# A 16-byte constant tile moved in front of the activations in SBUF

## The chip, the cores and the metric

One core of one Trainium2 chip. The metric is the device time of one execution in microseconds, lower is better; before the change the median of three runs is 929.96 us (928.1 to 932.1).

## The reference

A retention (linear attention) layer followed by two feed-forward layers, all in float32:

```python
scores = scale * np.matmul(q, k.transpose(0, 1, 3, 2))      # q, k, v: 4 x 8 x 576 x 64
ret = scores * Dmat[None]                                   # gamma[h] ** (i - j) for i >= j, else 0
x = np.matmul(ret, v)                                       # heads joined: x is 2304 x 512
h = x @ w_in;  g = np.maximum(0.01 * h, h);  x = g @ w_out      # first layer, d_ff = 2048
h = x @ w_in;  g = h - np.tanh(h);           x = g @ w_out      # second layer, own weights
```

## The kernel before

Everything lies in SBUF with 128 partitions. The activations are x, transposed, as two tensors: xh is x rounded to the matmul type fp32r, xl is what the rounding left. Each holds four slices (kk) of 128 features by 2304 tokens. The weights are split into a high and a low half in the same way, and so is g, the output of the elementwise part. One product therefore costs three matmuls: high x high, high x low, low x high.

The kernel first does the retention, in 16 pairs of heads, and fills xh and xl; meanwhile it already starts the first layer on narrow blocks of tokens. Then come the layers. Each has 16 slices of d_ff, in four groups of four; for a group the token blocks (four of 512 tokens and one of 256) are gone through, and for each block the four slices f. One (block, slice) is a step; there are 164 steps, 124 of them with 512 tokens. A step has

- `h_mm` (L181): 12 matmuls, over four kk and three pairs (w high, xh), (w high, xl), (w low, xh), all into one PSUM bank h. x is the moving operand, 512 or 256 columns; the weights of the ring are the stationary one.
- the elementwise part: `act_a` (L193, or L201 to L207 in the second layer) and `chain` (L215, or L218 to L222), then the split of g by ScalarE (L224) and GpSimd (L225).
- `o_mm` (L251): 12 matmuls of 512 columns into four PSUM banks, three for each, done LAG = 2 steps later. In the first layer g moves and the weights are stationary, in the second the weights move and g is stationary (there a block of 256 tokens takes 6 matmuls of 512 columns).
- after the fourth slice, `evac` (L276, L274): VectorE adds the banks to acc. At the end of a layer acc is split into xh and xl again (L280, L281), or stored.

The order of all instructions is written out by hand; in the loop of the layers a step issues h_mm(s), chain(s - 1), act_a(s), o_mm(s - 2), and between them the loads, the conversion of the next group's weights (lines 124 to 162) and the evictions. Within an engine the order is that of the code.

SBUF is laid out in the order in which tiles are taken from the pools. The pool `keep` comes first and holds xh, xl, acc and qb. xh, xl and acc have 36,864 bytes in each partition, 72 times 512. qb has 16 bytes in a slot of 32; it holds four constants that ScalarE's L204 and L207 use as bias. Behind `keep` come the ring of split weights (`wring`, two tags of four tiles of 4,096 bytes), the staging tiles, and the pools of a stage, with g in tiles of 4,096 bytes. In bytes from the partition's start:

```
tile          before   by 512      after   by 512
qb           127,104      128     16,512      128
xh            16,512      128     16,544      160
xl            53,376      128     53,408      160
acc           90,240      128     90,272      160
weight ring  127,136      160    127,136      160
g (layers)   188,576      160    188,576      160
```

Of the kernel before, what the change touches and what calls it, by code (L numbers as in the profile page):

```python
# [10 lines left out]
F32 = mybir.dt.float32  # L11
# [7 lines left out]
P = 128  # L19
# [14 lines left out]
def retention_moe_moe(  # L34
# [28 lines left out]
    keep = ctx.enter_context(tc.tile_pool(name="keep", bufs=1))  # L63
    wring = ctx.enter_context(tc.tile_pool(name="wring", bufs=GF))
    stage = ctx.enter_context(tc.tile_pool(name="stage", bufs=2))

    xh = keep.tile([P, KK, NT], F32R, name="xh")
    xl = keep.tile([P, KK, NT], F32R, name="xl")
    acc = keep.tile([P, KK * NT], F32, name="acc")
    acc_t = acc.rearrange("p (d t) -> p d t", d=KK)  # L70
    acc_n = acc.rearrange("p (t e) -> p t e", e=DM)
    qb = keep.tile([P, 4], F32, name="qb")

# [614 lines left out]
```

## Time and profile before

| | |
|---|---|
| median of three runs | 929.96 us (928.1 to 932.1) |
| the profiled execution's own time | 927.96 us |
| its span, first to last instruction | 926.1 us |
| mean granted clock of TensorE | 0.992 |
| PE busy | 886.5 us (96%), 4832 matmuls |
| VectorE, ScalarE, GpSimd busy | 597.6, 388.0, 468.5 us |
| HBM traffic | 57 MB, 62 GB/s over the span |

Times in the profile are those of one execution, from the span's start. PE is TensorE's matmuls, PEld its weight loads, DVE VectorE, ACT ScalarE, POOL GpSimd. A matmul's end is modelled and matmuls overlap in the records, so the pace of matmuls is read from the differences of their starts, not from durations. The chain of waits is followed back from the last instruction, at each step to what released it.

### The profile page before, as it was taken

What the parts mean: (1) busy time and instruction counts of PE and PEld (TensorE: products, weight loads), DVE (VectorE), ACT (ScalarE), POOL (GpSimd) and SP (SyncE); (2) the same over time, 40 slices, a digit from 0 to 9 for tenths busy, and PEclk for the clock granted to TensorE, in tenths of its full rate; (3) what the DMA queues carried; (4) which work ended last, traced back from release to release, by engine and by line L of the source; (5) the groups of instructions that cost most, each with busy time, mean ns of one, the idle gap of its engine ahead of it and who ended that gap; (6) DMA issues with size and microseconds to landing.
All of it is one profiled execution on the core that took longest, in us unless ns stands there. A gap on an engine that the chain in (4) does not pass through costs nothing.

```text
span 926.1 us, 12850 instructions
## 1 busy us (share of the span) xinstructions
PE 886.5 (96%) x4832; PEld 739.7 (80%) x4832; DVE 597.6 (65%) x988; ACT 388.0 (42%) x777; POOL 468.5 (51%) x364
## 2 busy tenths in 40 slices
PE   5777999999999999999999999999999999999998
PEld 5677888888888888888888787888888877888886
DVE  5887656656573655546762677758785877755544
ACT  2343332233222322233334555675456455575554
POOL 3544422245223523354646855586557645595444
PEclk9989999999999999999999999999999999999999
DMA  7654421211110011101110011101110011001111
GB/s 276 212 174 150 155 99 47 91 46 46 46 63 30 24 46 69 45 1 46 46 69 24 23 46 69 47 0 46 47 69 24 23 46 69 1 1 46 45 46 69
DMA packets 21662, 58.36 MB, mean 63 GB/s; under 512 B 2528, under 2 KB 2912, under 8 KB 21600
## 3 DMA queue, kind: packets, MB, share of 16 engines
q1 hardware_dynamic: 21024, 57.16, 17.9%
q8 instruction: 38, 0.62, 0.3%
q10 hardware_dynamic: 576, 0.38, 0.1%
q14 instruction: 24, 0.20, 0.1%
HBM read 52.81 MB, written 4.72 MB: 62 GB/s over the span
## 4 chain that ended last, share of the span: by engine, by line
PE 60%; DVE 17%; POOL 11%; issue 6%; ACT 5%; DMA 1%; DVEq 0%; POOLq 0%; ACTq 0%
PE a L251 29%; PE h L181 28%; POOL v L203 5%; POOL g L225 4%; DVE v L219 4%; DVE v L222 3%; ACT g L224 2%; DVE acc L276 2%; DVE st L430 2%; DVE pt L396 2%; PE o L459 2%; POOL wp L162 1%; DVE cw L139 1%; ACT xh L468 1%; DVE cw L134 1%
## 5 line engine op out<-in xcount | busy, mean ns | idle before, releaser
L181 PE MATMUL h<-xh,wp 128*128 128x512 f32 (+1 forms) x1216 | 377.0, 375 | 0.0
L181 PEld LDWEIGHTS h<-xh,wp 128*128 128x128 f32 x1216 | 223.2, 188 | 45.2
L181 PE MATMUL h<-xl,wp 128*128 128x512 f32 (+1 forms) x608 | 228.3, 375 | 0.0
L251 PE MATMUL a<-wp,g 128*128 128x512 f32 x864 | 213.4, 393 | 5.2 <-POOL g L225 5.0
L251 PE MATMUL a<-g,wp 128*128 128x512 f32 (+1 forms) x1008 | 216.3, 364 | 1.9 <-POOL g L225 1.9
L225 POOL TENSOR_TENSOR g<-a,g 128x512 fp32r<-128x512 f32 (+1 forms) x84 | 107.7, 1283 | 197.8 <-ACT g L224 197.8
L251 PEld LDWEIGHTS a<-g,wp 128*128 128x128 f32 x1008 | 173.6, 192 | 32.3 <-POOL g L225 2.1
L251 PEld LDWEIGHTS a<-wp,g 128*128 128x128 f32 x864 | 160.9, 188 | 43.8 <-POOL g L225 9.2
L225 POOL TENSOR_TENSOR g<-v,g 128x512 fp32r<-128x512 f32 (+1 forms) x80 | 104.0, 1299 | 142.2 <-ACT g L224 142.2
L181 PEld LDWEIGHTS h<-xl,wp 128*128 128x128 f32 x608 | 114.7, 189 | 22.2
L162 POOL TENSOR_TENSOR wp<-cw,wp 128x512 fp32r<-128x512 f32 x64 | 90.4, 1421 | 55.1 <-ACT wp L161 54.6
L145 DVE SCALAR_TENSOR_TENSOR cw<-st,cw 128x512 uint32<-128x512 uint32 x128 | 116.1, 907 | 3.0
L224 ACT ACTIVATE g<-v 128x512 fp32r<-128x512 f32 (+1 forms) x80 | 47.2, 590 | 163.6 <-DVE v L222 162.5
L193 ACT ACTIVATE a<-h 128x512 f32<-128x512 f32 (+1 forms) x72 | 40.4, 562 | 172.0 <-PE h L181 172.0
L215 DVE TENSOR_TENSOR a<-h,a 128x512 f32<-128x512 f32 (+1 forms) x72 | 46.3, 643 | 101.0 <-ACT a L193 101.0
L203 POOL TENSOR_TENSOR v<-t,u 128x512 f32<-128x512 f32 (+1 forms) x80 | 101.9, 1273 | 11.9 <-ACT t L202 11.8
L276 DVE TENSOR_TENSOR acc<-a,acc 128x512 f32<-128x512 f32 (+1 forms) x114 | 72.0, 659 | 51.9 <-PE a L251 51.8
L219 DVE SCALAR_TENSOR_TENSOR v<-q,v 128x512 f32<-128x512 f32 (+1 forms) x80 | 58.3, 728 | 59.0 <-POOL v L203 58.0
L218 DVE TENSOR_TENSOR h<-h,t 128x512 f32<-128x512 f32 (+1 forms) x80 | 51.2, 640 | 48.4 <-ACT t L202 48.4
L224 ACT ACTIVATE g<-a 128x512 fp32r<-128x512 f32 (+1 forms) x84 | 47.9, 570 | 80.7 <-DVE a L215 80.7
L139 DVE TENSOR_SCALAR cw<-cw 128x512 uint32<-128x512 uint32 x64 | 63.4, 991 | 1.5
L222 DVE COPY_PREDICATED v<-mk,h 128x512 f32<-128x512 uint32 (+1 forms) x80 | 55.1, 688 | 8.2
(56 smaller groups left out, 745.9 us busy)
## 6 DMA issues: line engine op xcount, KB each, us to landing
st<-in_w1i SPq DMA_DIRECT2D x16, 512.0 KB, 3.3
st<-in_w1o SPq DMA_DIRECT2D x16, 512.0 KB, 3.3
st<-in_w2i SPq DMA_DIRECT2D x16, 512.0 KB, 3.2
st<-in_w2o SPq DMA_DIRECT2D x16, 512.0 KB, 3.2
kv<-in_vn SPq DMA_DIRECT2D x16, 320.0 KB, 4.3
qk<-in_qT SPq DMA_DIRECT2D x16, 288.0 KB, 2.9
qk<-in_kT SPq DMA_DIRECT2D x16, 288.0 KB, 3.4
out<-acc SPq DMA_DIRECT2D x18, 256.0 KB, 2.1
```

The lines of the kernel that those rows point to most:

```text
L139: nc.vector.tensor_scalar(out=t["w"], in0=t["w"], scalar1=3, scalar2=0x3FFFFFF8, op0=ALU.logical_shift_left, op1=ALU.bitwise_and,)
L145: nc.vector.scalar_tensor_tensor(out=t["w"], in0=t[src], scalar=scalar, in1=t["w"], op0=op, op1=ALU.bitwise_or)
L162: nc.gpsimd.tensor_tensor(out=wp[:, 1, :], in0=wf, in1=wp[:, 0, :].bitcast(F32), op=ALU.subtract)
L181: nc.tensor.matmul(out=ps[:, :n], lhsT=w[:, wi, cs], rhs=x[:, kk, t0:t0 + n], start=kk == 0 and i == 0, stop=kk == KK - 1 and i == 2,)
L203: nc.gpsimd.tensor_tensor(out=v[:, :n], in0=t_[:, :n], in1=u[:, :n], op=ALU.mult)
L218: nc.vector.tensor_tensor(out=h, in0=h, in1=t_, op=ALU.subtract)
L219: nc.vector.scalar_tensor_tensor(out=v, in0=q, scalar=RHO_A, in1=v, op0=ALU.add, op1=ALU.mult)
L222: nc.vector.copy_predicated(out=v, mask=mk.bitcast(U32), data=h)
L224: nc.scalar.activation(out=gt[:, 0, :n], in_=v, func=AF.Copy)
L225: nc.gpsimd.tensor_tensor(out=gt[:, 1, :n], in0=v, in1=gt[:, 0, :n].bitcast(F32), op=ALU.subtract)
L251: nc.tensor.matmul(out=o, lhsT=l, rhs=r, start=f == 0 and i == 0 and d % pack == 0, stop=f == GF - 1 and i == 2 and (d + 1) % pack == 0, s ...
L276: nc.vector.tensor_tensor(out=dst, in0=a, in1=dst, op=ALU.add)
```

## The change

qb is taken from the pool first instead of last. Nothing else changes: same instructions, same order, same waits. xh, xl and acc begin 32 bytes further on, qb begins where xh began, and all that lies behind the pool keeps its place.

```diff
+    qb = keep.tile([P, 4], F32, name="qb")
     xh = keep.tile([P, KK, NT], F32R, name="xh")
     xl = keep.tile([P, KK, NT], F32R, name="xl")
     acc = keep.tile([P, KK * NT], F32, name="acc")
     acc_t = acc.rearrange("p (d t) -> p d t", d=KK)
     acc_n = acc.rearrange("p (t e) -> p t e", e=DM)
-    qb = keep.tile([P, 4], F32, name="qb")
```

## Rows read from the trace of the kernel before

**Rows 1.** The page: busy time of PE and others; clock by slices.
```profile
PE 886.5 (96%) x4832; PEld 739.7 (80%) x4832; DVE 597.6 (65%) x988; ACT 388.0 (42%) x777; POOL 468.5 (51%) x364
...
PEclk9989999999999999999999999999999999999999
```

**Rows 2.** The chain by line, three stretches: 152 to 300, 528 to 775, 773 to 926.
```profile
by line: PE a L251 50.2%; PE h L181 49.9%
...
by line: POOL v L203 18.6%; POOL g L225 12.7%; DVE v L219 12.5%; DVE v L222 11.3%; issue 11.0%; ACT g L224 8.0%; PE a L251 6.2%; PE h L181 4.8%; DVE acc L276 4.1%; POOL wp L162 3.1%; DVE cw L139 1.6%; DVE h L218 1.4%; DVE cw L134 1.1%; DVE 
...
by line: PE a L251 47.2%; PE h L181 46.7%; POOL g L225 1.7%; DVE acc L276 0.9%; POOL v L203 0.5%; issue 0.4%; ACT q L204 0.3%; ACT mk L207 0.3%; ACT u L201 0.3%; ACT g L224 0.2%; ACT t L202 0.2%; ACTq L201 0.0%; POOLq L225 0.0%
```

**Rows 3.** The chain, in order of time: start us, us, what. Hand-overs.
```profile
495.62 2.75 DVE acc L276 x4
...
535.34 2.79 PE a L251 x11
...
554.75 1.44 PE h L181 x12
...
773.33 1.43 PE a L251 x5
```

**Rows 4.** Timeline of PE, 402 to 410.5: start us, us, instructions merged.
```profile
402.04 2.91 PE L251 MATMUL a<-g,wp 128*128 128x512 f32 x12
404.78 0.40 PE L181 MATMUL h<-xh,wp 128*128 128x512 f32 x1
...
407.58 2.91 PE L251 MATMUL a<-g,wp 128*128 128x512 f32 x12
```

**Rows 5.** Timeline of PE, last matmuls of an o step, either layer.
```profile
403.65 1.30 PE L251 MATMUL a<-g,wp 128*128 128x512 f32 x5
...
787.38 1.30 PE L251 MATMUL a<-wp,g 128*128 128x512 f32 x5
788.51 0.40 PE L181 MATMUL h<-xh,wp 128*128 128x512 f32 x1
```

**Rows 6.** Counts of line L181: whole kernel; 152 to 496; 773 to 926.
```profile
L181 PE MATMUL h<-xh,wp 128*128 128x512 f32 x992 | 332.8, 397 | 0.0
...
L181 PE MATMUL h<-xh,wp x537: 277/396/628, 151.7 to 494.5; 128*128 128x512 f32 x147, 128*128 128x256 f32 x32
...
L181 PE MATMUL h<-xh,wp x224: 277/396/397, 774.6 to 916.0; 128*128 128x512 f32 x96, 128*128 128x256 f32 x16
```

**Rows 7.** Timeline of PE, steps of 256 columns, h and then o.
```profile
248.96 0.28 PE L181 MATMUL h<-xh,wp 128*128 128x256 f32 x1
...
250.38 0.86 PE L251 MATMUL a<-g,wp 128*128 128x512 f32 x3
...
261.55 1.60 PE L251 MATMUL a<-g,wp 128*128 128x256 f32 x12
262.99 0.40 PE L181 MATMUL h<-xh,wp 128*128 128x512 f32 x1
```

**Rows 8.** By line: ns min/median/max of VectorE and GpSimd, both remainders.
```profile
L276 DVE TENSOR_TENSOR acc<-a,acc x114: 414/691/692, 236.0 to 922.4; 128x512 f32<-128x512 f32 x102, 128x256 f32<-128x256 f32 x12
...
L215 DVE TENSOR_TENSOR a<-h,a x72: 410/691/694, 147.2 to 507.0; 128x512 f32<-128x512 f32 x60, 128x256 f32<-128x256 f32 x12
...
L281 POOL TENSOR_TENSOR xl<-acc,xh x20: 743/1302/1755, 437.6 to 524.7; 128x512 fp32r<-128x512 f32 x16, 128x256 fp32r<-128x256 f32 x4
...
L225 POOL TENSOR_TENSOR g<-a,g x84: 724/1290/1762, 49.0 to 510.0; 128x512 fp32r<-128x512 f32 x60, 128x256 fp32r<-128x256 f32 x24
```

**Rows 9.** Two waits of PE (idle us in brackets) and the clock after them.
```profile
463.93 2.33 PE L251 MATMUL a<-g,wp 128*128 128x256 f32 x11 [1.90 <-POOL g L225]
...
529.41 2.80 PE L251 MATMUL a<-wp,g 128*128 128x512 f32 x11 [1.01 <-POOL g L225]
...
464.40:467.80 3.40, 3.40 (x15) 3.01 (x14) 3.24 (x5) 0.42 (x1) 1.62 (x2) 0.50 0.41 152
528.00:532.00 4.00, 2.99 (x13) 2.17 (x12) 1.36 (x1) 0.00 (x0) 3.85 (x4) 1.00 0.38 128
```

## The prediction, made before the result was known

> **What bounds the kernel now.** I read the page first. TensorE (PE) is busy 96% of the span and its granted clock is 0.9 to 1.0 throughout, so the matmuls are the first suspect [rows 1]. The share is an average, though, and the change can only pay where PE is what ends last, so the second view is the chain of waits, cut into stretches. From 152 to 300 us it is PE alone, half L181 (the h matmuls, first product of a layer) and half L251 (the o matmuls, second product). From 528 to 775 us PE has 11% of it; the rest is the elementwise loop of the second layer, GpSimd (POOL) L203, VectorE (DVE) L219 and L222, ScalarE (ACT) L224, GpSimd L225, round and round. From 773 us it is PE again, 94% [rows 2]. The hand-overs can be seen in the chain: PE gives it up at 495.6 us to the eviction L276, and it is PE's again from 773.33 us [rows 3]. In between PE has the chain once more, from 535 to 555 us. So PE sets the end from 152 to 495 us and from 773 us on, about 490 us; before 152 us the retention stage has other limits and few wide matmuls.
>
> The third view is PE's own timeline in a stretch where nothing waits. An h step is 12 matmuls of 512 columns, an o step too. The h step that starts at 404.78 lasts until 407.58, 2.80 us, 0.233 a matmul. The o step from 402.04 lasts until 404.78, 2.74 us [rows 4]. Inside the o step the pace isn't even: the last five take 404.78 - 403.65 = 1.13 us, 0.226 each, so the first seven take 1.61 us, 0.230 each [rows 5]. A step of 12 at the fast pace is 2.72 us. Same shape, same data type, same alternation of two moving tiles, same granted clock, and no engine waited for: h pays 0.007 us a matmul more than o. What differs in the low bits of the addresses is that x begins at remainder 128 by 512, while weight ring and g both have 160. What could explain it otherwise and does not: h accumulates 12 matmuls into one PSUM bank and o three into each of four, but the last five of an o step contain both kinds of succession at one pace.
>
> **The change, part by part.** No instruction is added, taken away or reordered, and no wait changes. xh, xl and acc move up by the 32 bytes of the slot that qb had behind them; ring, staging, g and everything behind stay where they are.
>
> (1) h matmuls of 512 columns. At equal remainders the trace has no h, but it has o, whose moving and stationary operands both lie at 160 in either layer. Nearest rows: 0.226 at best, which would make an h step 2.72 us, 0.08 less. The other end: 256-column matmuls with equal remainders take 0.120 (the step from 261.55 to 262.99, 1.44 us), and two of these for 512 columns would be 0.240, an h step of 2.88 us, 0.08 more [rows 7]. I take 2.72: the o row has the shape in question, the 256-column row hasn't. h steps on PE's part of the chain: line L181 has 537 matmuls on xh from 152 to 496 us, 67 steps of 8 such matmuls, of which 12 are 256 columns wide, so 55; from 773 us 224 matmuls, 28 steps, 4 of them narrow, so 24 [rows 6]. 79 x 0.08 = 6.3 us. Bounds -6.3 and +6.3.
>
> (2) o matmuls. Only the first seven of a step are slow, the ones that follow h. If h keeps o's pace there is nothing left to recover from, and the step goes from 2.74 to 2.72; some 74 on the chain (as many as wide h steps, less a few that start fast already), 74 x 0.02 = 1.5 us. Bounds: -1.5 and 0, because their own addresses don't change.
>
> (3) Narrow h steps, 256 columns. Now 250.38 - 248.96 = 1.42 us at unequal remainders; o at equal ones 1.44 [rows 7]. Taken at 1.44: 19 on the chain (12, 4, and 3 around 555 us), 19 x 0.02 = +0.4 us. Bounds 0 and +0.4.
>
> (4) The other engines' reads and writes of xh, xl and acc. The same shapes stand in the trace at both remainders: DVE 0.691 us on acc (128) and 0.691 on a (160), POOL 1.302 on xl (128) and 1.290 on g (160), the median each [rows 8]. Nothing; the 18 stores of acc and the reads of qb keep their shape, and only the last store is not under matmuls.
>
> (5) What the rest of the time hides. The other 45 of the 124 wide h steps (992 matmuls on xh by 8 [rows 6]) lie between 495 and 773 us or before 152. Between 528 and 773 us the elementwise loop sets the pace and PE waits for it; there a faster PE only waits longer, and I count nothing. Around 535 to 555 us three h steps are on the chain, but the loop is as late there; 0.2 us.
>
> Sum: -6.3 - 1.5 + 0.4 - 0.2 = -7.6 us. All durations are from the profiled execution, 927.96 us (span 926.1 and 1.9 around it), which would become 920.4. The median of the runs is 929.96, 2.0 above, so I forecast 929.96 - 7.6, rounded 922.3 us. Without part (5) it would have been 124 x 0.10 = 12.4 us, 917.6: that is the mistake that the average share of PE invites.
>
> [...] The rows show a wide matmul at two paces, 0.233 and 0.226, at one granted clock [rows 4, 5]. [...]
>
> **The rivals.** A, the address isn't the cause, or only higher bits count. h stays at 0.233 and nothing moves: 930.0. For it: nothing in the trace varies x's remainder, so the reading above rests on one contrast, h against o, and the two also differ in tensor and in place. Against it: o ends at 0.226 with g moving in the first layer and also with weights moving in the second, 788.51 - 787.38 = 1.13 us for five [rows 5], and the 2.80 us of h go over both tensors and all four slices of x. Chance 0.17.
>
> B, h profits in part. After a change of operands o itself needs seven matmuls to reach its fast pace [rows 5]. If every step starts so, an h step comes to today's o step, 2.74: 79 x 0.06 = 4.7 us, nothing from (2), 925.6 with (3). For it: that slow start is what one sees now. Against: it could be left over from h. Chance 0.12.
>
> C, slower: equality itself costs. The 256-column rows have the sign the wrong way round, 1.44 equal against 1.42 unequal [rows 7]. If the wide h followed them, up to 0.240 a matmul, it would be +6.3 + 0.4, 936.7. It turns into a loss from 0.2335 on and into one that can be told from none at 0.238. Against it: wide o at equal remainders never settles there. Chance 0.05.
>
> D, the waits tip the clock. [...] Waits between 528 and 773 us grow with a faster PE, about 4 us over a dozen of them. Each that is followed by half clock costs about 3.4/2 = 1.7 us; five take the whole gain (930.8), eight make it slower (935.9). Chance 0.04.
>
> **How the numbers follow.** The forecast has 0.62. Within it single terms can be off (1 us in the count of steps on the chain, 2 us in the median of the runs): 919.3 to 924.8. What a measurement can tell from no change is about 0.5%, 4.65 us: faster means under 925.3, slower over 934.6. Faster: nearly all of the forecast, 0.58, and half of B, 0.06, together 0.64. Slower: C 0.05 and half of D 0.02, together 0.07. Same: what is left, 0.29. For 8 in 10 the range takes in the forecast, B, and the lower part of A (its runs spread from 928.1 to 932.1): 919 to 929.3, about 0.6 + 0.12 + 0.07. C, D and the rest of A stay outside.
>
> **What would show it.** Right: in PE's timeline an h step of 2.72 us instead of 2.80 and an o step of 2.72 with no slow start; from 152 to 495 us the same steps end about 5.5 us sooner; from 528 to 773 us the stretch keeps its length and PE waits more for L225; after it PE's steps are short again. Wrong: h steps of 2.80 (A), 2.74 with slow starts (B), above 2.80 (C), more stretches at half clock (D). If the stretch from 528 to 773 us also shortens, part (5) was wrong and the gain goes towards 12 us.

## The result: 920.0 us, and the profile after

The changed kernel takes 920.0 us (median of five runs, 919.2 to 923.8) beside 929.96 for the kernel before (five runs, 927.4 to 932.1): ratio 0.9906, 95% interval 0.9885 to 0.9926. The forecast was 922.3, range 919.0 to 929.3. The profiled execution took 922.67 us, its span is 920.9.

The pages first (after). PE is as busy as before, 95% against 96% [rows 1], so the average share tells nothing of the gain.

```profile
PE 878.9 (95%) x4832; PEld 742.5 (81%) x4832; DVE 597.6 (65%) x988; ACT 388.2 (42%) x777; POOL 468.2 (51%) x364
...
PEclk9987999999999999999999999999999999999999
```

PE's timeline shows the gain (after; start us, us, instructions merged), in the stretch that answers to [rows 4]:

```profile
400.88 2.88 PE L251 MATMUL a<-g,wp 128*128 128x512 f32 x12
403.60 0.39 PE L181 MATMUL h<-xh,wp 128*128 128x512 f32 x1
...
406.32 0.84 PE L251 MATMUL a<-g,wp 128*128 128x512 f32 x3
```

From start to start the o step is 403.60 - 400.88 = 2.72 us and the h step 406.32 - 403.60 = 2.72, where they were 2.74 and 2.80 [rows 4]. That is 0.227 a matmul all through; the slow first seven [rows 5] are gone. Steps of 256 columns, which answer to [rows 7] (after, timeline of PE):

```profile
249.80 0.28 PE L181 MATMUL h<-xh,wp 128*128 128x256 f32 x1
...
251.24 2.91 PE L251 MATMUL a<-g,wp 128*128 128x512 f32 x12
253.98 0.28 PE L181 MATMUL h<-xh,wp 128*128 128x256 f32 x1
...
259.60 1.60 PE L251 MATMUL a<-g,wp 128*128 128x256 f32 x12
...
261.04 0.28 PE L181 MATMUL h<-xh,wp 128*128 128x256 f32 x1
```

The narrow h step is 251.24 - 249.80 = 1.44 us (others 1.43; before 1.42), the narrow o step 1.44 as before. The wide o step behind a narrow h still takes 253.98 - 251.24 = 2.74, so the slow start is left there alone.

Now where it counts. The chain's hand-overs, which answer to [rows 3]; first the kernel before at the start of its PE stretch, then after at both ends (start us, us, what):

```profile
152.10 2.73 PE a L251 x12
```

```profile
154.76 2.72 PE a L251 x12
...
493.21 2.74 DVE acc L276 x4
...
770.57 1.42 PE a L251 x5
```

| stretch | before | after | change | forecast |
|---|---|---|---|---|
| first wide o step on the chain to L276 | 343.5 | 338.5 | -5.1 | -5.3 |
| to the last wait of the second layer | 277.7 | 277.4 | -0.3 | -0.1 |
| to the end of the span | 152.8 | 150.3 | -2.5 | -2.3 |
| sum | 774.0 | 766.1 | -7.9 | -7.6 |

(The forecast's column splits its terms by their counts: 55, 24 wide h steps and as many o steps, 12, 3 and 4 narrow ones. The forecast took five o steps fewer, so its sum is 0.1 smaller.) The retention stage ahead of it is 2.7 us longer in this profile; the experiments come to that. PE's waits, which the forecast wanted to grow, before and then after (us in total, times, longest):

```profile
PE a L251 <- POOL g L225: 6.9, 9, 1.9
```

```profile
PE a L251 <- POOL g L225: 9.3, 13, 1.9
```

Where the gain goes in the second layer is best read by laying step starts of both kernels side by side. Timeline of PE, before and then after; the same four steps in each fence (the o step ahead of the narrow steps in the second layer's second group, the first o step between narrow steps, the next wide h step, an o step late in the third group):

```profile
653.44 2.91 PE L251 MATMUL a<-wp,g 128*128 128x512 f32 x12
657.61 2.91 PE L251 MATMUL a<-wp,g 128*128 128x512 f32 x12
...
671.62 0.40 PE L181 MATMUL h<-xh,wp 128*128 128x512 f32 x1
...
732.70 2.91 PE L251 MATMUL a<-wp,g 128*128 128x512 f32 x12
```

```profile
649.10 3.34 PE L251 MATMUL a<-wp,g 128*128 128x512 f32 x12
...
653.71 0.39 PE L251 MATMUL a<-wp,g 128*128 128x512 f32 x1
654.47 2.79 PE L251 MATMUL a<-wp,g 128*128 128x512 f32 x11 [0.37 <-POOL g L225]
...
668.86 0.39 PE L181 MATMUL h<-xh,wp 128*128 128x512 f32 x1
...
728.78 3.22 PE L251 MATMUL a<-wp,g 128*128 128x512 f32 x12
```

After's lead on before is 653.44 - 649.10 = 4.34 us at the first of these, 671.62 - 668.86 = 2.76 at the third, 732.70 - 728.78 = 3.92 at the fourth, and at the hand-over 773.33 - 770.57 = 2.76 again. So PE does gain 0.10 a pair of steps in the middle of the layer too, and gives all of it back: mostly at the narrow steps, where the waits on L225 are, and also at wide ones, as in the steps at 728.78 us, whose record is stretched to 3.22, and at 734.56, which lose 0.32 and 0.43. The chain by line, cut as in [rows 2] (after):

```profile
by line: PE h L181 50.3%; PE a L251 49.9%
...
by line: PE h L181 27.6%; PE a L251 25.3%; POOL v L203 8.6%; DVE v L219 6.5%; DVE v L222 6.2%; POOL g L225 6.2%; issue 5.9%; ACT g L224 4.0%; DVE acc L276 3.1%; DVE cw L139 1.7%; DVE h L218 1.3%; DVE cw L134 0.9%; DVE acc L274 0.8%; DVE cw 
...
by line: PE a L251 47.4%; PE h L181 46.4%; DVE acc L276 0.9%; POOL g L225 0.7%; ACT q L204 0.5%; ACT u L201 0.5%; ACT mk L207 0.5%; ACT t L202 0.4%; issue 0.3%; ACT g L224 0.2%; ACTq L201 0.0%
```

The middle line is a trap. PE has 53% of that chain after and had 11% before, yet the stretch kept its length. The chain takes whichever path ended last, by hundredths of a microsecond: after, an L203 at 613.93 us starts 0.02 behind the end of a PE step; before, the same L203 at 616.67 came behind GpSimd's own work, and the two lie 2.74 apart, the lead of the whole loop. Of two paths that tie, the shares don't say which to shorten; the length of the stretch does.

### The profile page after: what moved, and what is told of

It reads as the page before. It is cut to its first block, busy times and chain, and to the rows that moved or that the text cites. A ratio compares the mean times of both kernels' runs of the same rounds, so it can differ in the third digit from the quotient of the medians.

```text
span 920.9 us, 12850 instructions
## 1 busy us (share of the span) xinstructions
PE 878.9 (95%) x4832; PEld 742.5 (81%) x4832; DVE 597.6 (65%) x988; ACT 388.2 (42%) x777; POOL 468.2 (51%) x364
## 4 chain that ended last, share of the span: by engine, by line
PE 73%; DVE 12%; POOL 6%; issue 4%; ACT 3%; DMA 1%; DVEq 0%; ACTq 0%; POOLq 0%; SPq 0%
PE a L251 34%; PE h L181 33%; POOL v L203 2%; POOL g L225 2%; PE o L459 2%; DVE v L219 2%; DVE v L222 2%; DVE acc L276 2%; DVE pt L396 2%; DVE st L430 1%; ACT g L224 1%; DVE cw L139 1%; PE x_a L447 1%; DVE cw L134 1%; DVE cw L145 1%
## 5 line engine op out<-in xcount | busy, mean ns | idle before, releaser
L181 PE MATMUL h<-xh,wp 128*128 128x512 f32 (+1 forms) x1216 | 370.6, 370 | 0.0
L181 PEld LDWEIGHTS h<-xh,wp 128*128 128x128 f32 x1216 | 223.4, 189 | 39.8
L181 PE MATMUL h<-xl,wp 128*128 128x512 f32 (+1 forms) x608 | 225.1, 370 | 0.0
L225 POOL TENSOR_TENSOR g<-a,g 128x512 fp32r<-128x512 f32 (+1 forms) x84 | 107.9, 1285 | 193.3 <-ACT g L224 193.3
L251 PEld LDWEIGHTS a<-wp,g 128*128 128x128 f32 x864 | 160.4, 188 | 45.8 <-POOL g L225 13.3
L225 POOL TENSOR_TENSOR g<-v,g 128x512 fp32r<-128x512 f32 (+1 forms) x80 | 103.9, 1299 | 142.1 <-ACT g L224 142.1
L181 PEld LDWEIGHTS h<-xl,wp 128*128 128x128 f32 x608 | 114.8, 189 | 19.9
L203 POOL TENSOR_TENSOR v<-t,u 128x512 f32<-128x512 f32 (+1 forms) x80 | 102.0, 1275 | 9.6 <-ACT t L202 9.5
L276 DVE TENSOR_TENSOR acc<-a,acc 128x512 f32<-128x512 f32 (+1 forms) x114 | 71.6, 658 | 49.8 <-PE a L251 49.8
```

The costliest lines, as they stand in the source:

```text
L181: nc.tensor.matmul(out=ps[:, :n], lhsT=w[:, wi, cs], rhs=x[:, kk, t0:t0 + n], start=kk == 0 and i == 0, stop=kk == KK - 1 and i == 2,)
L203: nc.gpsimd.tensor_tensor(out=v[:, :n], in0=t_[:, :n], in1=u[:, :n], op=ALU.mult)
L225: nc.gpsimd.tensor_tensor(out=gt[:, 1, :n], in0=v, in1=gt[:, 0, :n].bitcast(F32), op=ALU.subtract)
L251: nc.tensor.matmul(out=o, lhsT=l, rhs=r, start=f == 0 and i == 0 and d % pack == 0, stop=f == GF - 1 and i == 2 and (d + 1) % pack == 0, s ...
L276: nc.vector.tensor_tensor(out=dst, in0=a, in1=dst, op=ALU.add)
```

## The experiments

Two questions: is it the place of x against the weights (theory E, equality) or x's own place (P), or is h slow for a reason of its own (H); and is the gain between 528 and 773 us hidden by the elementwise loop (part 5)? Below, "from first o" is the time from the start of the first wide o step on the chain's first stretch to the end of the span: before 774.2 us, after 766.3 (0.2 more than in the table, since the chain takes that step up 0.16 us behind its first matmul). It leaves the retention stage out.

**All at 128.** Against the kernel before; x stays at 128, ring and g come to 128.

```diff
-    qb = keep.tile([P, 4], F32, name="qb")
+    qb = keep.tile([P, 128], F32, name="qb")
```

> x, weight ring and g all begin at remainder 128 by 512 (qb last again, in a slot of 512 bytes). Theory E, equality: what counts is that moving and stationary operand begin alike, wherever that is. Then h and o steps of 512 columns both take 2.72 us and the kernel about 920 us, as after the change. Rival P, place: 160 is a good place for a moving operand and 128 a bad one. Then h steps take 2.80 us, o steps 2.80 too (g now moves from 128), and the kernel about 934 us. If the change's gain came from neither, h stays at 2.72 or 2.80 with no link to o.

920.31 us, ratio 0.9894 (0.9875 to 0.9914); from first o 766.2. Timeline of PE:

```profile
301.17 2.88 PE L251 MATMUL a<-g,wp 128*128 128x512 f32 x12
303.89 0.39 PE L181 MATMUL h<-xh,wp 128*128 128x512 f32 x1
...
306.61 2.88 PE L251 MATMUL a<-g,wp 128*128 128x512 f32 x12
```

2.72 and 2.72. x at its old place is as fast as at the new one: P falls.

**Only the ring and g at 128.** On top of the change, so x at 160, ring and g at 128.

```diff
     acc = keep.tile([P, KK * NT], F32, name="acc")
+    pad0 = keep.tile([P, 120], F32, name="pad0")
```

> x at 160 as after the change, weight ring and g at 128: the inequality of before turned round. Theory E: h steps 2.80 us again, o steps 2.74 (equal at 128, but disturbed after h), about 929 us. Rival P: h 2.72 us (x moves from 160), o 2.80 in the first layer (g moves from 128) and in the second (weights move from 128), about 926 us.

930.78 us, ratio 1.0005 (0.9989 to 1.002). Timeline of PE (the pad shifts line numbers by one):

```profile
300.03 2.92 PE L252 MATMUL a<-g,wp 128*128 128x512 f32 x12
302.79 0.40 PE L182 MATMUL h<-xh,wp 128*128 128x512 f32 x1
...
305.59 2.92 PE L252 MATMUL a<-g,wp 128*128 128x512 f32 x12
```

The whole gain is gone, with x where the change put it: o 2.76, h 2.80. Rival A and P are out, and E holds: what counts is x against the ring, 0.233 us a matmul in h where they begin 32 bytes apart and 0.227 where they begin alike. Whether the matmul or the weight load is held up, the runs don't tell.

**x 64, 256 and 128 bytes away.** On top of the change; qb wider and a pad behind acc, so that ring and g stay at 160.

```diff
-    qb = keep.tile([P, 4], F32, name="qb")
+    qb = keep.tile([P, 24], F32, name="qb")     # [P, 72], [P, 40]
...
+    pad0 = keep.tile([P, 112], F32, name="pad0")  # [P, 64], [P, 96]
```

> x at 224, ring and g at 160: a distance of 64 bytes. Theory E by 512, as the change words it: h 2.80 us, about 929 us. Theory E by 64 or by 32: h 2.72 us, about 920 us. Rival P (32 past a multiple of 64 is a good place): h 2.72 us, 920 us.

> x at 416, ring and g at 160: a distance of 256 bytes. Theory E by 512: h 2.80 us, about 929 us. Theory E by 256, 128 or 64: h 2.72 us, about 920 us. Rival P: 2.72 us, 920 us. Together with the distance of 64 this tells which bits of the address count.

> x at 288, ring and g at 160: a distance of 128 bytes. A distance of 256 was harmless and one of 64 cost 0.04 us a step. Theory E by 128: h 2.72 us. Theory E by 256: h above 2.74 us.

At 64 bytes 929.06 us, ratio 0.9997 (0.9984 to 1.0011); at 256 bytes 920.53, ratio 0.989 (0.9871 to 0.991); at 128 one run without repeats, 931.65. Timelines of PE, in that order:

```profile
300.42 0.40 PE L182 MATMUL h<-xh,wp 128*128 128x512 f32 x1
...
303.19 2.93 PE L252 MATMUL a<-g,wp 128*128 128x512 f32 x12
305.96 0.40 PE L182 MATMUL h<-xh,wp 128*128 128x512 f32 x1
```

```profile
302.47 0.39 PE L182 MATMUL h<-xh,wp 128*128 128x512 f32 x1
...
305.19 2.88 PE L252 MATMUL a<-g,wp 128*128 128x512 f32 x12
307.91 0.39 PE L182 MATMUL h<-xh,wp 128*128 128x512 f32 x1
```

```profile
300.94 2.90 PE L252 MATMUL a<-g,wp 128*128 128x512 f32 x12
303.68 0.40 PE L182 MATMUL h<-xh,wp 128*128 128x512 f32 x1
...
306.47 2.90 PE L252 MATMUL a<-g,wp 128*128 128x512 f32 x12
```

h is 2.77, 2.72 and 2.79; o 2.77, 2.72, 2.74. So 256 bytes away is as good as 0, and 32, 64 and 128 are not: equality by 256 is enough, by 128 it is not. At 64 bytes h is quicker than at 32, yet the kernel is not: the o step behind it, whose own operands still begin alike, takes 2.77 instead of 2.74, so the pair is 5.54 us again. The slow start isn't a fixed cost; it depends on the step before.

**Only g at 128.** On top of the change; g alone is moved away from the ring.

```diff
+            gp = mc.enter_context(tc.tile_pool(name="gp", bufs=1))
+            pad0 = gp.tile([P, 120], F32, name="pad0")
```

> The change with g alone moved to 128; x and weight ring stay at 160. The penalty should move from h to o. Theory E: h steps 2.72 to 2.74 us; o steps 2.80 in the first layer (moving operand g 32 below the stationary one, as x was) and about 2.76 to 2.80 in the second (weights move, 32 above g). On the chain of before that is some 76 o steps at +0.06 to 0.08 against the change, 924 to 927 us. Rival H, that h itself was slow for another reason (one PSUM bank for 12 matmuls, the tensor x) and the shift of x only mended it by chance: o stays at 2.72 to 2.74, 920 us.

928.6 us, ratio 0.9991 (0.9975 to 1.0007). Timeline of PE, first layer and then second:

```profile
300.23 2.96 PE L251 MATMUL a<-g,wp 128*128 128x512 f32 x12
303.03 0.39 PE L181 MATMUL h<-xh,wp 128*128 128x512 f32 x1
...
305.77 2.96 PE L251 MATMUL a<-g,wp 128*128 128x512 f32 x12
...
854.25 2.95 PE L251 MATMUL a<-wp,g 128*128 128x512 f32 x12
...
857.05 0.39 PE L181 MATMUL h<-xh,wp 128*128 128x512 f32 x1
```

Now o is the slow one, 2.80 in the first layer and 2.79 to 2.80 in the second, whichever of g and the weights moves. In the first layer h has 2.74, the slow start that o used to have (in the second 2.72 to 2.73). H falls. The expected time was missed: it priced o alone and left out that the step behind a slow one starts slowly, the term (2) of the forecast seen from the other side. That is an estimated 1.1 us over the 55 wide h steps of the first layer's stretch; what the rest is, no run divides.

**The second layer with the first layer's light elementwise part.** Both conditions `m == 0`, in act_a and in chain, become true, so that these two kernels leave out h - tanh(h); once with the new order of tiles, once with the old.

```diff
-        if m == 0:
+        if True:
```

> The changed kernel with the second layer's elementwise part replaced by that of the first (the larger of h and 0.01 h instead of h - tanh(h)): five elementwise instructions a step less on ScalarE, VectorE and GpSimd. To be compared with the next one, which has the layout of before. Part 5 of the prediction (the elementwise loop of the second layer hides the gain between 528 and 773 us): without that loop the gain rises from 7.6 to about 11 us. Rival: the gain there is lost to something that this kernel keeps (evictions, weight conversion, loads): it stays at 7 to 8 us.

> The kernel before with the same replacement of the second layer's elementwise part: the other half of the comparison. h steps 2.80, o steps 2.74 us; PE without waits between 528 and 773 us, so some 8 us below the kernel before (its waits for g there), about 921 us, and 11 us above the one with the new layout if part 5 holds, 7 to 8 above it otherwise.

910.36 us with the new order, 921.32 with the old: 10.96 apart. The medians alone would not show that this is more than the 8 to 10 us of the kernels with the loop in place, since the two ratios' intervals combine to some 3 us either way. The profiles do: from first o 752.6 and 766.0, 13.3 apart, against 7.9. Of the 13.3, 1.6 us are the clock's. Both kernels, like before and after, have a wait of PE of 1.9 us for L225 in the first layer (at 461.75 us in the new order, 467.01 in the old), and in the old order alone a stretch at half clock follows. Windows view, old order and then new (stretch us, busy us of PE, PEld, DVE, ACT, POOL with counts, granted clock, DMA share, GB/s):

```profile
455.00:475.00 20.00, 18.09 (x107) 16.19 (x106) 13.73 (x20) 6.03 (x13) 9.54 (x8) 0.91 0.16 55
```

```profile
455.00:475.00 20.00, 18.15 (x115) 16.28 (x114) 15.75 (x24) 7.87 (x17) 12.90 (x12) 1.00 0.15 53
```

Before and after both have 0.91 there, so their 7.9 is like with like; here 11.7 us are left for the change of tiles. In the second layer the windows view (new order) has PE busy in all of the stretch, with the clock at 1.00:

```profile
528.00:775.00 247.00, 247.00 (x1158) 207.33 (x1157) 135.31 (x196) 70.62 (x127) 89.68 (x68) 1.00 0.14 45
```

The 11.7 us lie close to the 12.4 that the forecast gave for the case without part (5). The part stands: take the loop away and the steps between 528 and 773 us give their share as well.

**Earlier issue of act_a in the second layer.** Can the hidden share be had without lightening the loop? It now issues act_a(s) before chain(s - 1), so that ScalarE takes up the new h ahead of its split of the step before: in all of the second layer, with the new and the old order of tiles.

```diff
-                tight = s >= end - GF
+                tight = s >= end - GF or steps[s][0] == 1
```

> The changed kernel, and in the second layer every step issues act_a(s) before chain(s - 1), as its last four steps do already. GpSimd then has the product L203 of step s before the split L225 of step s - 1, and the elementwise loop (L203, L219, L222, L224, L225, L203 of the next step) is broken: each link waits for PE's h instead. By part 5 the stretch from 528 to 773 us then becomes PE's, its waits go, and the kernel takes about 910 us, as with the cheap elementwise part. Rival: the loop is not broken but turned round (ScalarE's split now waits behind act_a, g comes later), PE waits at each step of 256 columns, and it is 918 us or above.

> The same reordering on the kernel before, without the move of qb. If it frees PE, about 921 us, 11 us above the one with the move, as in the pair with the cheap elementwise part; the two edits then add up to more than each alone (8 to 9 each). If it doesn't, 928 us or above.

920.23 us, ratio 0.9911 (0.9877 to 0.9946), and 929.57, ratio 1.0023 (0.9997 to 1.0048). Both times that were expected if PE came free were missed, and the rivals' bounds (918 us or above, 928 or above) held: no gain over the change, and none over the kernel before. In the new order PE has 87% of the chain from 528 to 775 us, but it still waits for L225 eleven times, 7.7 us in all (after: 13 times, 9.3 us), and the layer's entry costs more. Timeline of PE, after and then this kernel (idle us in brackets), and this kernel's windows view behind that wait:

```profile
526.70 2.83 PE L251 MATMUL a<-wp,g 128*128 128x512 f32 x11 [1.34 <-POOL g L225]
```

```profile
528.02 3.84 PE L251 MATMUL a<-wp,g 128*128 128x512 f32 x11 [3.55 <-POOL g L225]
```

```profile
529.50:532.90 3.40, 3.40 (x9) 2.63 (x8) 3.33 (x4) 0.54 (x1) 2.99 (x3) 0.50 0.00 0
```

The wait is 2.2 us longer, and this time half clock follows it, as rival D has it; in after, with the same tiles, the wait of 1.34 us was not followed by it (clock 1.00 from 528 to 775 us).

From first o it still has 763.7, 2.6 less than after, against 774.8 with the old order, none. But 1.6 of the 2.6 are again the clock's, since the wait at 462.59 us isn't followed by half clock here as it is in after; 1.0 is left, and the times don't show it.

**The same in the middle of the layer alone, and the change once more.** The earlier order only for steps 96 to 135, which leaves the layer's entry (step 84 on) as it is; and the changed kernel unedited.

```diff
-                tight = s >= end - GF
+                tight = s >= end - GF or 96 <= s < 136
```

> The changed kernel with the early act_a only in steps 96 to 135 of the 164, that is from the first layer-two block after the narrow ones up to the last narrow block of the third group. In the run with the early act_a everywhere in layer two these two groups were 1.4 and 2.4 us shorter than with the change alone, but the entry into layer two 2.2 us longer and the last group 0.8 longer. If these add, 3.5 to 4 us below the change: 916 to 917 us, 1.3% below the kernel before. If the two orders don't join without a wait, 919 us or above.

> The change as it is, once more, beside the two. 7 to 9 us below the kernel before, about 921 us; steps of 2.72 us, h and o alike. The retention stage, 2.7 us longer in the profile of the change than in that of before, should fall anywhere between 149 and 155 us, if that was chance; if the change makes it longer, 154 us or above again.

The first takes 915.93 us, ratio 0.9866 (0.9845 to 0.9887): it beats both kernels. From first o 760.6, 5.7 less than after; 1.6 of that is the clock's once more (1.00 from 455 to 475 us, where after has 0.91), and 4.1 are the edit's, about as many as the medians show (920.22 and 915.93). Its waits on L225 and its chain by line from 528 to 775 us:

```profile
PE a L251 <- POOL g L225: 6.4, 11, 1.9
```

```profile
by line: PE h L181 41.0%; PE a L251 39.1%; POOL g L225 4.6%; POOL v L203 2.8%; issue 2.3%; DVE v L222 2.1%; DVE v L219 1.8%; ACT g L224 1.7%; ACT u L201 0.9%; DVE cw L128 0.7%; DVE cw L139 0.6%; DVE h L218 0.5%; ACT t L202 0.5%; ACT q L204 
```

Here PE's larger share comes with a shorter stretch. The changed kernel once more took 920.22, ratio 0.9923 (0.9895 to 0.9951); from first o 766.1, steps 2.72. But its first wide o step came at 157.1 us, outside the 149 to 155 that chance was given, and on the side of "the change makes retention longer". In the fourteen profiles the step came between 151.9 and 157.6 us: with x, ring and g as before at 151.9, 152.7 and 155.0, as the change has x and the ring at 152.3, 154.4, 154.6, 155.3, 155.7 and 157.1, in the other layouts between 153.4 and 157.6. The ranges overlap, and the granted clock goes with the time. Windows view of before, of the kernel just above (x where the change has it) and of the repeat:

```profile
0.00:152.00 152.00, 123.27 (x1317) 111.62 (x1318) 103.65 (x274) 49.06 (x145) 63.67 (x57) 0.97 0.49 163
```

```profile
0.00:152.00 152.00, 122.72 (x1315) 111.34 (x1316) 103.43 (x273) 48.98 (x145) 63.22 (x57) 0.97 0.50 163
```

```profile
0.00:152.00 152.00, 123.38 (x1294) 112.91 (x1295) 98.73 (x267) 48.22 (x143) 62.22 (x56) 0.91 0.49 163
```

The clock is third from the right, a mean over stretches at 1.00 and stretches at 0.50, the two levels that [rows 9] show. At 0.97 the step came at 151.9 in the old layout and 152.3 in the new; at 0.93 at 152.7 and 155.0 in the old and 154.6 in the new (after); at 0.91 in the repeat at 157.1. After and the repeat are one program and differ by 2.5 us here. So it is the spread of that stage, and the layers' gain is the same 7.9 to 8.1 in both.

## Why the prediction was right

- **What bounds, and the counts.** The cut of the chain into stretches was right, and so were the steps counted in each: -5.1, -0.3 and -2.5 us against -5.3, -0.1 and -2.3.
- **(1) Wide h, -0.08 each.** Measured 2.80 to 2.72. The reason, equality with the ring, is shown by moving either side: x back at 128 with the ring there is fast, x at 160 with the ring at 128 is slow. The reading was too narrow in one point: it had to be equal by 512, and by 256 is enough.
- **(2) o, -0.02 each.** Measured 2.74 to 2.72. That the slow start is inherited from the step before, and is no cost of every change of operands, is shown by o behind narrow h steps (2.74 still), by h behind slow o steps (2.74, with g at 128), and by o steps of 2.74, 2.76 and 2.77 that had equal operands of their own behind h steps at different distances. This is what separates the forecast from rival B.
- **(3) Narrow h, +0.02.** Measured 1.42 to 1.43 or 1.44. Rival C had read this sign rightly and would have spread it to the wide steps, which went the other way. (Its break-even of 0.2335 us a matmul is 0.2329 by its own sum; nothing hangs on that.)
- **(4) Other engines, nothing.** Their busy times are 597.6, 388.2 and 468.2 us, against 597.6, 388.0 and 468.5.
- **(5) Hidden in the second layer.** Right in size: the stretch gave 0.3 us, and with the loop lightened the same change of tiles is worth 11.7 in the profiles. The forecast said that PE only waits longer there. The trace says more exactly that it runs ahead by up to 1.6 us and gives that back, mostly at the narrow steps.
- **Rival D.** The waits grew by 2.4 us, where it had put 4, and the stretch stayed at clock 1.00. What it named was seen: a wait of 3.55 us at the second layer's entry in the reordered kernel was followed by 3.40 us at clock 0.50, and one such stretch cost 1.6 us where it had estimated 1.7, half of the 3.40 us in [rows 9].

The one loose term was the base. The forecast set its -7.6 on the median of before; the ratio's interval is -6.9 to -10.7 us, and the traces have -7.9. What the median shows beyond that, 2.1 us, is within the noise: the repeat's medians differ by 8.1 us (928.28 and 920.22), and over all runs that have a span on record, 57 of before and 12 of the change, the mean spans are 927.3 and 919.3 us, 8.0 apart, or 7.9 (give or take 0.8) if the runs are compared at like mean clock. So the sum of -7.6 was right to 0.3 us, and most of the 2.3 us by which the forecast lay above the median is that noise, not a term of the sum.

Open: why the place matters inside the chip. The runs show that the distance between the starts of the moving and the stationary operand counts; they don't show which unit minds it. Distances other than 0, 32, 64, 128 and 256 weren't run.

## What to carry to other kernels

Where two matmul lines of one shape run at different paces with nothing waited for, compare the starts of their operands modulo 256 bytes (here 0.227 us a matmul at 0 and 256 bytes apart, 0.231 to 0.233 at 32, 64 and 128); a small tile in front of large ones can shift all of them, and here moving it added no instruction. Price a faster engine by stretches that it alone ends, not by its share, and expect the rest back as waits at the stretch's thinnest steps (here PE's waits on L225 grew from 6.9 to 9.3 us, and the stretch from 495 us to the last wait gave 0.3). If the chain's shares change but a stretch's length doesn't, two paths tie: loosen the other one, and only where it binds, as the early act_a showed, which was worth nothing that the times show over the whole layer and 4 us in its middle. Before two profiles are compared, compare their clock stretch by stretch: one stretch at half clock made 1.6 us of difference between kernels that ran alike up to it.

## What the runs showed of the chip

- A matmul with 512 columns of fp32r took 0.227 us where moving and stationary operand start 0 or 256 bytes apart (modulo 512), 0.233 at 32, 0.231 at 64 and 0.233 at 128 (h steps of 2.72, 2.80, 2.77 and 2.79 by 12). With 256 columns the sign is the other way, 0.118 at 32 and 0.119 to 0.120 at 0.
- The matmuls behind a slow or a narrow step start slowly, though their own operands are equal: 0.230 for the first seven on average in before. It costs 0.02 us a step there, 0.04 with ring and g at 128 and 0.05 with x 64 bytes away (steps of 2.74, 2.76 and 2.77 against 2.72).
- One and the same wait of PE, 1.8 to 1.9 us long, between 459 and 469 us, was followed by 3.4 us at half clock in eight of the fourteen profiles and stayed at full clock in six. It cost 1.6 us: in before the eleven narrow o matmuls and the h step behind the wait took 466.06 - 463.93 = 2.13 and 469.66 - 466.06 = 3.60 us instead of 1.32 (11 by 0.120) and 2.80.
- The first wide o step came between 151.9 and 157.6 us in fourteen profiles of kernels whose retention stage is the same, with the granted clock of the first 152 us between 0.97 and 0.90. That is 0.6% of the whole, so that one profile's span can hide a change of this size.
